# The token sums of the second pair made by VectorE alone, with another table of shifted steps, in a two-layer attention and SwiGLU kernel

## The chip, the core and the metric

The kernel runs on one core of one Trainium2 chip. The metric is the device time of one execution in microseconds (us). Five engines work beside each other on queues of their own: TensorE (PE in the profile; PEld is its weight load), VectorE (DVE), ScalarE (ACT), GpSimd (POOL) and SyncE (SP), which here only issues DMAs.

## What is computed

Two layers, each an attention block with a compressive memory and then a SwiGLU feed-forward block, on 2048 tokens of width 512 in float32. Cut to what matters here:

```python
def _B_ref(x, w_gate, w_up, w_down):      # 512 -> 1792 -> 512
    g = _silu(x @ w_gate)
    u = x @ w_up
    return (g * u) @ w_down
x = x + _A_ref(_layernorm(x), ...)        # attention, four segments of 512 tokens, 32 heads
x = x + _B_ref(_layernorm(x), ...)
x = x + _A_ref(_layernorm(x), ...)
x = x + _B_ref(_layernorm(x), ...)
```

## The kernel before

**Numbers in two parts.** Every operand of a large matmul is held as a rounded part hi and a rest lo; a product is the three matmuls hi·hi, lo·hi and hi·lo, summed in one PSUM bank.

**The feed-forward block** (`ffn`) cuts the 2048 tokens into four blocks of 512 and takes them as two pairs, m = 0 (blocks 0 and 1) and m = 1 (blocks 2 and 3, the "second pair"). The 1792 columns are seven chunks of 256. Chunk 0 is done plainly (`up`, matmuls in line 1039); chunks 1 to 6 are done by a Strassen-Winograd scheme (`strassen`, matmuls in line 1069) that makes seven products in place of eight. Three of its products take the tokens as they are; the other four need sums and differences of token blocks, T0 to T3. These are the **token sums**: `make_t(m)` makes them once for each pair, and all six chunks use them. `down` (matmuls in line 1113, added to the running result in line 1118) multiplies a finished chunk by the down weights.

**The token sums.** `make_t` runs `one(kc)` twice, for the two halves kc of the contraction. Each time it makes T2 (a difference of two parts of block 1 of the pair, three elementwise instructions in `diff`, tiles xn), T0 (three, tiles tt), T1 (two, tile of) and T3 (two, tile tt), all of 128x512 float32 in line 983 for the profile, and then splits each of them in `spl`: ScalarE copies the hi part (line 1004) and VectorE subtracts it to get the lo part (line 1005). `T3E = ("dve", "pool")` says who makes T2: VectorE for the first pair, GpSimd for the second. `strassen` asks for T1 first (`prod(PY, a, 1, tk(1))`, the second product), for T2 two products later. The first matmuls on T1 need its hi part for both kc, the last two its lo part.

**The order of the work.** No engine chooses at run time: each executes its queue in order. The program collects all 13816 operations (`Program.op`) with a price and a due time, `P.prio`; then `issue` runs a list schedule twice (`walk`). In the first walk each engine takes, of its operations whose inputs are ready by the plan, the one with the least due time, the earlier index at a tie. The start that comes out is shifted by `NUDGE[index]` for the operations that the table names, and the second walk takes these as due times and emits the queues. The planner's price of one 512-column VectorE instruction is 512/960 + 0.0687 = 0.602 us; that of a GpSimd token-sum instruction is 1.29 us. It knows no slowdown of one engine by another. All operations of one `make_t(m)` have the same due time, `v + TAT[m]`, so ties go by index: T2, T0, T1, T0's split, T3, then the splits of T1, T3 and T2.

**Around it in the second pair**: block 3 is normed and transposed (line 407; parts hi and lo in lines 411 and 412); its `up` matmuls (line 1039) run while the token sums are made; `down(0, 2)` and `down(0, 3)` (chunk 0 of blocks 2 and 3) have a later due time than the first Strassen chunk; `load_s` prepares the next weights, with sums in line 922 and lo parts in line 936 on GpSimd and hi parts in line 935 on ScalarE. `P.hold` makes the next layer's first norm wait for the VectorE instructions of `make_t(1)`.

Of the kernel before, what the change touches and what calls it, by code (L numbers as in the profile page):

```python
# [24 lines left out]
NB = 3  # L25
CAP = {'pj': 3, 'plt': 3, 'pmx': 3, 'ppv': 3, 'ff': 6, 'st': 6}
LPW = 3
NUDGE = {60: 2.9, 61: -0.9, 124: 0.3, 137: 0.3, 141: -3.3, 171: 4.0, 210: -0.7, 375: 18.2, 377: 15.8, 523: 13.7,
# [7 lines left out]
WOT = ("st", "st", "pj", "pj")  # L36
EARLY_AT = (23, 25, 26)
PAIR, STEP, WAT, TAT = 11.852, 7.441, 15.217, (16.363, 16.627)
T3E = ("dve", "pool")
FIN = 4.95  # L40
WQ1 = -11.849
TA, TF = 15.0, 16.7
# [12 lines left out]
    dve=dict(dve=0.13, act=0.12, pe=0.2, pool=0.17, sp=0.12),  # L55
    pool=dict(pool=0.1, dve=0.14, pe=0.12, act=0.13, sp=0.05),
# [31 lines left out]
class Program:  # L88
# [70 lines left out]
    def issue(self):  # L159
# [11 lines left out]
        for o in self.ops:  # L171
            o.prio = o.start + NUDGE.get(o.index, 0.0)
        self.walk(True)
# [100 lines left out]
def infini_swiglu(ctx: ExitStack, tc: tile.TileContext, x, wq, wk, wv, wo, beta, wg, wu, wd, out,  # L274
# [4 lines left out]
    pool = ctx.enter_context(tc.tile_pool(name="sb", bufs=1))  # L279
# [6 lines left out]
    def sb(tag, shape, dtype=F32, ring=1):  # L286
        return P.buf(pool, tag, shape, dtype, ring)
# [14 lines left out]
    def act(n, fn, reads, writes, sbuf=False, table=None):  # L302
        op("act", n / 1200 + (0.093 if sbuf else 0.05), fn, reads, writes).table = table

    def dve(n, fn, reads, writes, fast=1):
        op("dve", n / 960 / fast + 0.0687, fn, reads, writes)

    def gp(cost, fn, reads, writes):
        op("pool", cost, fn, reads, writes)
# [559 lines left out]
    def ffn(base, x_in, x_out, slots, T):  # L869
# [97 lines left out]
        def make_t(m):  # L967

            (h0, l0), (h1, l1) = XT[2 * m], XT[2 * m + 1]
            R = [sb(slots[f"t{k}"], [128, 2, 4, 2, 128], F32R) for k in range(4)]  # L970
            TT.update(enumerate(R))

            def one(kc):
                half = lambda b, k: (b, lambda: b.ap[:, :, 2 * k + kc].bitcast(F32))
                raws = {}

                def tmp(tag):
                    raw = sb(tag, [128, 4, 128])
                    return raw, lambda: raw.ap

                def ew(eng, f, out, x, y):
                    g = nc.vector if eng == "dve" else nc.gpsimd
                    fn = lambda: getattr(g, f)(out[1](), x[1](), y[1]())  # L983
                    if eng == "dve":
                        dve(512, fn, [x[0], y[0]], [out[0]])
                    else:
                        gp(1.29, fn, [x[0], y[0]], [out[0]])

                def diff(k, eng, tags, ha, la, a, hb, lb, b):
                    d, r = tmp(tags[0]), tmp(tags[1])  # L990
                    ew(eng, "tensor_sub", d, half(ha, a), half(hb, b))
                    ew(eng, "tensor_sub", r, half(la, a), half(lb, b))
                    ew(eng, "tensor_add", r, r, d)
                    raws[k] = r

                def less(k, tag, ha, la, a, j):
                    r = raws[k] = tmp(tag)
                    ew("dve", "tensor_sub", r, half(ha, a), raws[j])
                    ew("dve", "tensor_add", r, r, half(la, a))

                def spl(k):
                    b, r = raws[k]
                    hi, lo = [lambda a=a: R[k].ap[:, a, :, kc] for a in range(2)]
                    act(512, lambda: nc.scalar.copy(hi(), r()), [b], [(R[k], (0, kc))], sbuf=True)  # L1004
                    dve(512, lambda: nc.vector.tensor_sub(lo(), r(), hi().bitcast(F32)),  # L1005
                        [b, (R[k], (0, kc))], [(R[k], (1, kc))])
                diff(2, T3E[m], ("xn_2", "xn_3"), h1, l1, 1, h1, l1, 0)
                diff(0, "dve", ("tt_0", "tt_1"), h1, l1, 0, h0, l0, 0)
                less(1, "of", h1, l1, 1, 0)
                spl(0)  # L1010
                less(3, "tt_0", h0, l0, 1, 1)
                for k in (1, 3, 2):
                    spl(k)
            one(0)
            one(1)

        nup, last = [0], []
# [252 lines left out]
```

## Time and profile before

| | us |
|---|---|
| median of 3 runs | 1867.84 |
| lowest and highest run | 1866.89, 1871.88 |
| the profiled execution | 1871.46 |
| its span, first to last instruction | 1869.7 |
| PE busy | 1822.9 |
| DVE busy | 1407.8 |
| POOL busy | 931.9 |

The profiled execution lies 1.76 us over its own span and 3.62 us over the median of the three runs. Rows of the trace give times from the start of the span. A timeline row gives the start, the time from the start of the first to the end of the last instruction that it merges, the engine, the line and, in brackets, how long the engine sat idle before and whom it waited for.

### The profile page before, as it was taken

To read this page: it belongs to the slowest core of one execution; us is meant where nothing else is said; L and a number is where in the kernel's file an instruction comes from. 1 tells how busy PE (TensorE), PEld (TensorE's weight loads), DVE (VectorE), ACT (ScalarE), POOL (GpSimd) and SP (SyncE) were. 2 spreads that over 40 slices of the span, in tenths; PEclk is the share of its full clock that TensorE was granted. 3 is DMA by queue.
4 is the path that set the end of the run, shared out by engine and by line. 5 is a ranking of instruction groups with operands and counts; after the bars stand their busy time and mean duration, and the time that the engine had idled before them with its cause. 6 is when DMAs were issued, how large, how long until landed. Compare 5 with 4: busy or idle time off the path is not lost.

```text
span 1869.7 us, 33023 instructions
## 1 busy us (share of the span) xinstructions
PE 1822.9 (97%) x11360; PEld 1450.5 (78%) x11360; DVE 1407.8 (75%) x3822; ACT 870.1 (47%) x1629; POOL 931.9 (50%) x1196
## 2 busy tenths in 40 slices
PE   7999999999999999999999999999999999989999
PEld 5787787877778877888877878777777788868887
DVE  6878788788876669766786777887898765786656
ACT  4565564555533343434345655555554433333432
POOL 6344444444655556646533444454345646464551
PEclk9999999999999999999999999999999999999999
DMA  7435444464232122111373354455642312321111
GB/s 240 145 103 148 140 133 141 145 207 128 74 119 63 45 84 92 57 51 52 102 237 103 104 165 117 128 173 146 201 110 76 116 47 58 95 68 51 45 57 46
DMA packets 126967, 206.14 MB, mean 110 GB/s; under 512 B 14160, under 2 KB 52048, under 8 KB 126800
## 3 DMA queue, kind: packets, MB, share of 16 engines
q1 hardware_dynamic: 124752, 203.49, 36.5%
q8 instruction: 91, 1.49, 0.4%
q10 hardware_dynamic: 2048, 0.53, 0.1%
q14 instruction: 76, 0.62, 0.1%
HBM read 136.34 MB, written 67.11 MB: 109 GB/s over the span
## 4 chain that ended last, share of the span: by engine, by line
PE 81%; DVE 9%; DMA 3%; issue 2%; POOL 2%; ACT 2%; SPq 1%; DVEq 0%; POOLq 0%; ACTq 0%
PE ps L1069 24%; PE ps L315 16%; PE ps L1113 15%; PE ps L578 8%; PE ps L629 7%; PE ps L656 7%; PE ps L1039 2%; DVE tt L983 1%; DVE junk L584 1%; PE ps L407 1%; DVE s L1005 1%; PE ps L710 1%; DMA ck<-scrk 1%; DVE s L1118 1%; DMA s<-nm 1%
## 5 line engine op out<-in xcount | busy, mean ns | idle before, releaser
L1069 PE MATMUL ps<-s,s 128*128 128x512 f32 x2016 | 542.5, 396 | 11.9 <-ACT s L1004 6.9
L315 PE MATMUL ps<-s,s 128*128 128x512 f32 x1536 | 523.1, 407 | 3.5 <-ACT s L471 1.8
L584 DVE CUSTOM_DVE_ANT_0 junk<-ps,amask 128x128 bf16<-128x128 f32 (+3 forms) x1024 | 433.9, 484 | 42.2 <-PE ps L578 40.6
L1069 PEld LDWEIGHTS ps<-s,s 128*128 128x128 f32 x2016 | 376.5, 188 | 107.1 <-ACT s L1004 8.7
L1113 PE MATMUL ps<-s,vt 128*128 128x512 f32 x1296 | 376.6, 397 | 1.1 <-ACT vt L1025 1.1
L315 PEld LDWEIGHTS ps<-s,s 128*128 128x128 f32 x1536 | 286.9, 190 | 52.7 <-issue 6.4
L635 ACT ACTIVATE s<-ps 128x512 f32<-128x512 f32 x448 | 254.2, 611 | 107.7 <-PE ps L629 95.8
L1113 PEld LDWEIGHTS ps<-s,vt 128*128 128x128 f32 x1296 | 245.6, 190 | 58.0 <-ACT vt L1025 1.5
L578 PE MATMUL ps<-ck,s 127*128 127x256 f32 (+2 forms) x1024 | 279.3, 334 | 4.4 <-DMA ck<-scrk 1.1
L629 PE MATMUL ps<-s,ck 128*128 128x256 f32 x1280 | 252.1, 288 | 4.1 <-DMA s<-nm 2.5
L629 PEld LDWEIGHTS ps<-s,ck 128*128 128x128 f32 x1280 | 220.7, 189 | 36.8 <-issue 3.9
L1118 DVE TENSOR_TENSOR s<-s,ps 128x512 f32<-128x512 f32 x224 | 149.8, 682 | 95.1 <-PE ps L1113 94.9
L639 POOL TENSOR_SCALAR_AFFINE_SELECT s<-s 128x512 f32<-128x512 f32 x192 | 128.2, 669 | 172.2 <-ACT s L635 169.6
L578 PEld LDWEIGHTS ps<-ck,s 127*128 127x128 f32 x1024 | 178.4, 189 | 28.4 <-issue 4.4
L936 POOL TENSOR_TENSOR s<-mem,s 128x512 fp32r<-128x512 f32 x96 | 130.0, 1354 | 0.2 <-ACT s L935 0.2
L1039 PE MATMUL ps<-s,s 128*128 128x512 f32 x384 | 122.2, 399 | 0.4 <-ACT s L411 0.4
L943 POOL COPY turn<-vt 128x1 f32<-128x1 f32 x20 | 3.7, 184 | 237.1 <-DVE vt L1026 237.1
L512 POOL TENSOR_SCALAR s<-raw 128x512 fp32r<-128x512 f32 x64 | 41.0, 640 | 161.1 <-ACT raw L511 159.6
L656 PE MATMUL ps<-s,vt 128*32 128x384 f32 (+3 forms) x1536 | 115.7, 419 | 0.3 <-DVE mx L584 0.2
L656 PEld LDWEIGHTS ps<-s,vt 128*32 128x32 f32 x1536 | 43.4, 109 | 64.7 <-issue 48.0
L635 ACT ACTIVATE pc<-ps 128x512 f32<-128x512 f32 x128 | 79.1, 619 | 20.5 <-PE ps L629 18.8
L514 POOL TENSOR_TENSOR s<-raw,s 128x512 fp32r<-128x512 f32 x64 | 84.0, 1312 | 4.4
(173 smaller groups left out, 2599.2 us busy)
## 6 DMA issues: line engine op xcount, KB each, us to landing
s<-scrq SPq DMA_DIRECT2D x128, 192.0 KB, 3.6
ck<-scrk SPq DMA_DIRECT2D x128, 192.0 KB, 4.5
scrq<-s SPq DMA_DIRECT2D x32, 512.0 KB, 3.9
scrk<-s SPq DMA_DIRECT2D x32, 512.0 KB, 3.4
scrq<-s SPq DMA_DIRECT2D x32, 256.0 KB, 3.3
scrk<-s SPq DMA_DIRECT2D x32, 256.0 KB, 2.4
s<-xmid SPq DMA_DIRECT2D x32, 256.0 KB, 4.7
xin<-xmid SPq DMA_DIRECT2D x32, 256.0 KB, 2.6
```

Source lines behind the costliest of these rows:

```text
L315: pe(n, passes, lambda: nc.tensor.matmul(view(ps.ap), lhsT=av(a.ap), rhs=bv(b.ap), start=start, stop=stop), [(a, rk[0]), (b, rk[1])], [ps])
L578: nc.tensor.matmul(ps.ap[:, a * 256:a * 256 + nk], lhsT=cq.ap[0:127, 2 * j + p, qt * 128:(qt + 1) * 128], rhs=ck.ap[0:127, p, 0:nk], start ...
L584: dve(w, lambda a=a, qt=qt, w=w, ps=ps, junk=junks[qt % 2]: nc.vector.tensor_tensor_reduce(out=junk.ap[:, :w], in0=ps.ap[:, a * 256:a * 25 ...
L629: nc.tensor.matmul(ps.ap[:, 256 * p:256 * p + 256], lhsT=ck.ap[:, p, kt * 128:kt * 128 + 128], rhs=cq.ap.rearrange("r (j p) c -> r p j c", ...
L635: act(512, lambda: nc.scalar.activation(view().rearrange("p x i c -> p (x i c)"), ps.ap, AF.Exp, scale=SCALE), [ps], [(Pb, key)], table="exp")
L639: gp(0.593, lambda: nc.gpsimd.affine_select(out=view()[:, 0], in_=view()[:, 0], pattern=[[0, 4], [1, 128]], compare_op=OP.is_ge, fill=0.0, ...
L656: nc.tensor.matmul(ps.ap[32 * i:32 * i + 32, qt * 128:(qt + k) * 128], lhsT=vt.ap[:, kt, VW * hd:VW * hd + 32], rhs=view(k=k)[:, :, idx], ...
L936: gp(n / 400, lambda hi=hi, lo=lo, src=src: nc.gpsimd.tensor_sub(lo(), src(), hi().bitcast(F32)), [read, (wt, (o0, 0))], [(wt, (o0, 1))])
L1039: pe(512, 1, lambda i=i, j=j, kc=kc, x=x, ps=ps, wt=wt: nc.tensor.matmul(ps.ap, lhsT=wt.ap[:, i, kc, cs], rhs=XT[b][j].ap[:, :, kc], start ...
L1069: pe(512, 1, lambda i=i, kc=kc, x=x, buf=buf, view=view: nc.tensor.matmul(ps.ap, lhsT=w.ap[:, o, i, kc], rhs=view(buf.ap, kc), start=(x == 0),
L1113: pe(512, 1, lambda i=i, j=j, fi=fi, x=x, ps=ps, wt=wt, cs=cs: nc.tensor.matmul(ps.ap, lhsT=ht.ap[:, 0:2048].rearrange("p (f a c) -> p f a ...
L1118: dve(512, lambda ps=ps, t=t: nc.vector.tensor_add(xb.ap[:, t, :], xb.ap[:, t, :], ps.ap), [ps, (xb, t)], [(xb, t)])
```

## The change

All four token sums of the second pair are made by VectorE, as those of the first pair are: the six GpSimd instructions of each `make_t(1)` (three for each kc, twelve in the two layers) become VectorE instructions in the planner's and the engine's queue. The operations and their indices stay the same. The table of shifts is another one: 70 entries in place of 69, with three indices in common (2909, 6986 and 13792). Neither table names an operation of `make_t(1)`. Since a shift changes what the planner puts next, the queues of all engines can differ from the first shifted operation on.

```diff
-NUDGE = {60: 2.9, 61: -0.9, 124: 0.3, 137: 0.3, 141: -3.3, 171: 4.0, 210: -0.7, 375: 18.2, 377: 15.8, 523: 13.7,
...
-         11949: -3.0, 12102: 7.2, 13281: -4.5, 13432: 7.2, 13635: -0.5, 13792: 12.4}
+NUDGE = {74: 4.6, 103: 0.2, 106: -2.3, 127: -8.8, 159: 2.0, 161: 2.9, 194: -0.8, 269: 5.1, 313: 23.9, 370: 1.3,
...
+         11776: -0.5, 11827: 3.5, 12216: 0.7, 12218: 10.1, 12451: 5.3, 13590: 10.5, 13792: 10.4}
-T3E = ("dve", "pool")
+T3E = "dve"
...
-                diff(2, T3E[m], ("xn_2", "xn_3"), h1, l1, 1, h1, l1, 0)
+                diff(2, T3E, ("xn_2", "xn_3"), h1, l1, 1, h1, l1, 0)
```

## Rows read from the trace of the kernel before

**Rows 1.** The page, part 1: busy time and share of each engine.

```profile
PE 1822.9 (97%) x11360; PEld 1450.5 (78%) x11360; DVE 1407.8 (75%) x3822; ACT 870.1 (47%) x1629; POOL 931.9 (50%) x1196
```

**Rows 2.** Busy time by stretch: length, engines, granted clock (PEclk), DMA share, GB/s.

```profile
0.00:60.00 60.00, 45.36 (x197) 35.99 (x198) 39.65 (x135) 28.15 (x51) 32.43 (x56) 0.97 0.71 220
...
715.00:755.00 40.00, 35.93 (x149) 27.87 (x148) 35.86 (x46) 13.25 (x25) 26.61 (x21) 0.91 0.25 86
755.00:925.00 170.00, 170.00 (x743) 137.61 (x742) 117.42 (x189) 68.01 (x120) 95.50 (x114) 1.00 0.21 63
...
1640.00:1680.00 40.00, 34.55 (x149) 27.17 (x148) 35.39 (x46) 13.03 (x24) 26.32 (x21) 0.96 0.22 74
```

**Rows 3.** Timeline of PE around the second pair's first Strassen products, first layer.

```profile
729.35 8.92 PE L1039 MATMUL ps<-s,s 128*128 128x512 f32 x38
...
740.43 0.86 PE L1069 MATMUL ps<-s,s 128*128 128x512 f32 x3
744.22 2.57 PE L1069 MATMUL ps<-s,s 128*128 128x512 f32 x8 [2.93 <-ACT s L1004]
747.55 1.22 PE L1069 MATMUL ps<-s,s 128*128 128x512 f32 x2 [0.76 <-DVE s L1005]
748.57 4.96 PE L1113 MATMUL ps<-s,vt 128*128 128x512 f32 x13
753.37 0.40 PE L1069 MATMUL ps<-s,s 128*128 128x512 f32 x1
```

**Rows 4.** Timeline of PE at the same place of the second layer.

```profile
1665.17 0.85 PE L1069 MATMUL ps<-s,s 128*128 128x512 f32 x3
1668.71 2.13 PE L1069 MATMUL ps<-s,s 128*128 128x512 f32 x8 [2.69 <-ACT s L1004]
1673.17 0.73 PE L1069 MATMUL ps<-s,s 128*128 128x512 f32 x2 [2.32 <-DVE s L1005]
1673.73 4.74 PE L1113 MATMUL ps<-s,vt 128*128 128x512 f32 x13
1678.31 0.40 PE L1069 MATMUL ps<-s,s 128*128 128x512 f32 x1
```

**Rows 5.** Busy time of 2 us behind the waits of the first layer (columns of Rows 2).

```profile
748.00:750.00 2.00, 2.00 (x6) 1.52 (x6) 1.32 (x3) 0.74 (x2) 0.08 (x1) 0.50 0.00 0
```

**Rows 6.** Timeline of DVE around the token sums, first layer, then second layer.

```profile
721.98 0.68 DVE L1026 TENSOR_TENSOR vt<-raw,vt 128x512 fp32r<-128x512 f32 x1
...
725.57 2.61 DVE L983 TENSOR_TENSOR tt<-s,s 128x512 f32<-128x512 f32 x2
728.22 1.67 DVE L983 TENSOR_TENSOR tt<-tt,tt 128x512 f32<-128x512 f32 x1
729.81 1.27 DVE L1118 TENSOR_TENSOR s<-s,ps 128x512 f32<-128x512 f32 x2
...
742.84 0.68 DVE L983 TENSOR_TENSOR of<-of,s 128x512 f32<-128x512 f32 x1
...
744.57 1.78 DVE L983 TENSOR_TENSOR tt<-s,of 128x512 f32<-128x512 f32 x1
746.28 1.22 DVE L1005 TENSOR_TENSOR s<-of,s 128x512 fp32r<-128x512 f32 x1
...
1650.31 2.38 DVE L983 TENSOR_TENSOR tt<-s,s 128x512 f32<-128x512 f32 x2
...
1667.33 0.68 DVE L983 TENSOR_TENSOR of<-of,s 128x512 f32<-128x512 f32 x1
```

**Rows 7.** Timeline of POOL in the same stretch.

```profile
727.71 1.63 POOL L983 TENSOR_TENSOR xn<-xn,xn 128x512 f32<-128x512 f32 x1
...
743.15 0.95 POOL L936 TENSOR_TENSOR s<-phik,s 128x256 fp32r<-128x256 f32 x1 [3.19 <-ACT s L935]
```

**Rows 8.** Group by line, POOL's subtractions of the token sums: busy, mean ns, idle before.

```profile
L983 POOL TENSOR_TENSOR xn<-s 128x512 f32<-128x512 f32 x8 | 13.7, 1713 | 13.3 <-ACT s L1004 10.0 <-ACT s L411 2.8 <-DVE s L412 0.3
```

**Rows 9.** Timeline of PE in the first pair, first layer: the wait for a token sum.

```profile
539.63 1.66 PE L1069 MATMUL ps<-s,s 128*128 128x512 f32 x6 [0.65 <-ACT s L1004]
```

12 rows, old and new, of the table NUDGE are left out of this document.

## The prediction

> **What bounds the kernel now.** I read the page's busy shares first: TensorE is busy 97% of the span, the next engine 75% [rows 1]. So the end is set by TensorE's work and by what little it idles, 1869.7 - 1822.9 = 46.8 us. The busy time by stretch then says where that idle time lies: 14.6 us at the start (60.00 - 45.36), 4.1 us in the 40 us around the second pair's token sums of the first layer, 5.5 us in the same stretch of the second layer, and nothing in the 170 us that follow [rows 2]. Because TensorE is full behind it, a microsecond won in one of these stretches is a microsecond off the end. The same rows show a second thing: the granted clock is 1.00 in the full stretch, but 0.91 and 0.96 in the two with the token sums. So those stretches cost more than their idle time.
>
> **What the two stretches cost.** I take the timeline of TensorE there. With full queues a matmul of 512 columns, 0.40 us long, starts every (8.92 - 0.40)/37 = 0.230 us, from the 38 at 729.35 [rows 3]. In the first layer three matmuls from 740.43 are through their issue at 741.12; TensorE then waits for ScalarE's hi part of T1, later for VectorE's lo part of it, and reaches the matmul at 753.37. In those 12.25 us it issued 8 + 2 + 13 = 23 matmuls, worth 5.29 us: 7.0 us are lost [rows 3]. In the second layer the same count from 1665.86 to 1678.31 gives 12.45 - 5.29 = 7.2 us [rows 4]. Part of it is not waiting: behind the waits of the first layer the granted clock is 0.50, the lower of the two levels, 1.2 in place of 2.4 GHz, and the matmuls of the down product run at half pace until it rises [rows 5]; in the second layer the stretch has 0.96 [rows 2]. Together the two places hold 14.1 us (6.96 + 7.16), 0.75% of the span.
>
> **Why T1 is late.** Next the timeline of VectorE. It is busy for 35.9 of the 40 us [rows 2]. T1's last sum for kc = 1 begins at 742.84 as the 22nd instruction of the row, 17.27 us after the first [rows 6]. Two undisturbed instructions of 0.68 us, the pair at 729.81, take 1.27 us together [rows 6], so one starts some 0.60 us after the other, and 21 starts need 12.6 us. The other 4.7 us are in instructions that ran while GpSimd made T2: 2.61 us for two and 1.67 us for one that takes 0.68 us alone [rows 6], beside GpSimd's 1.63 us from 727.71 on [rows 7]. In the second layer the 22nd instruction begins at 1667.33, 17.02 us after the first, an excess of 4.4 us [rows 6]. After that, T3's sum and T1's lo part take 1.78 and 1.22 us [rows 6] beside GpSimd's weight work, which starts at 743.15 [rows 7] and stays.
>
> **The change part by part.**
> *Removed:* twelve GpSimd instructions, of which the eight subtractions alone are 13.7 us, of an engine half idle [rows 1, 8]. By themselves they are worth nothing; what goes with them is VectorE's excess of 4.7 and 4.4 us.
> *Added:* six VectorE instructions in each layer ahead of T1, because T2 has the lower index: 6 x 0.60 = 3.6 us. They stand before the two additions of line 1118 and before the split of block 3's activations; those come at most 3.6 us later by count and about 1 us earlier in time. Net on VectorE's chain: T1's hi part comes 4.7 - 3.6 = 1.1 us earlier in the first layer and 0.8 us in the second. ScalarE's copies and the next layer's first norm wait for the same last instruction as now, so `P.hold` costs nothing.
> *The plan:* this is the larger part. By its own prices the planner had T1's hi part ready for TensorE at 725.57 + 12.6 + (744.22 - 742.84) = 739.6 [rows 3, 6], before TensorE was done with its other work at 741.1, so it saw no gap and put nothing into it; on the chip it came at 744.2. After the change the planner expects 739.6 + 3.6 = 743.2, and its 0.602 us is the chip's 0.60 us with GpSimd out of the way. It sees 2.1 us missing and fills them, nine matmuls, with what is ready. There is plenty: the down product of chunk 0 for block 2 is 48 matmuls, 11 us, and its last input is written at 721.98 + 0.68 us [rows 6]. Then T1's hi part no longer stalls TensorE. If that cover were absent, 2.1 us of waiting would stay, plus the clock.
> *What is late next:* T1's lo part, behind T3's sum and GpSimd's weight work. Its bounds are 0 (the fill also moves the lo part's matmuls back) and the 2.32 us that TensorE waited for it in the second layer [rows 4]. The nearest row is the first pair, where VectorE makes all four sums already and TensorE waits 0.65 us [rows 9]; I take 1.0 us in each layer, and no fall of the clock.
> Sum of this part: 7.0 + 7.2 - 2 x 1.0 = 12.1 us off (from 14.1).
>
> What the trace shows of the two engines together is that VectorE's sums of two SBUF tiles take 1.67 to 1.78 us beside GpSimd and 0.68 us alone [rows 6, 7]. The Trainium skill has a rule for it in "SBUF — State Buffer", section "Who interferes with whom": a VectorE instruction with two SBUF inputs contends with a GpSimd instruction that reads SBUF, and one with a single SBUF input does not. That speaks against the change too, since all instructions that it gives to VectorE are of the contending kind and GpSimd's weight work remains; the second rival below is priced for that.
>
> *The table.* No shift, old or new, is on an operation of `make_t(1)`, but the queues are drawn anew from the first one. The trace of before shows no row for the new order. The bounds come from what there is to win or lose: in the first 60 us TensorE idles 14.6 us [rows 2], of which no order removes the wait for the first rows; I allow 5 us of gain there and in the small waits of the rest. A loss has a price in [rows 3, 4]: a wait of some 3 us that pulls the clock down costs 7 us. I take 0, as nothing in the rows tells one table from the other.
>
> **From span to time.** The sum is against the profiled 1871.46 us, which lies 3.62 us over the median of the three runs; the runs spread by 5 us. Against its own time the change gives 1871.5 - 12.1 = 1859.4; against the median 1867.84 - 12.1 = 1855.7. Since a profiled execution that is slower than the median may have lost more to the clock than the others did, I take 1 us less of gain: 1857.
>
> **The rivals.**
> *1. The forecast:* both stalls go but for about 1 us, the table is neutral: 1857, own range 1853 to 1862. Chance 0.45.
> *2. The contention moves on.* GpSimd's weight work meets the longer row of VectorE sums, T1's lo part stays 2.3 us late in each layer and the clock still falls, which costs the 7.2 - 2.69 - 2.32 = 2.2 us of the second layer [rows 4]: 14.1 - 2 x 4.5 = 5.1 us won, 1863. For it: the 1.78 and 1.22 us beside the weight work [rows 6]. Against it: the planner's fill moves the matmuls on T1 back by 2.1 us. Chance 0.2. The skill's rule named above would give this case if all the remaining GpSimd instructions met a VectorE sum.
> *3. The table also mends the start and the rest:* 12 + 5 us, 1851. Against it: the rows give no reason. Chance 0.15.
> *4. Slower: the new order opens stalls elsewhere.* Outside the first 60 us and the two stretches TensorE idles only 46.8 - 14.6 - 4.1 - 5.5 = 22.6 us in 1730 us now, in many small pieces [rows 1, 2]; an order that lets it wait some 3 us at a place would drop the clock and cost 7 us there, as in [rows 3, 4]. Two such places eat the 12 us; with the third the kernel is slower than before, 1867.8 - 12 + 21 = 1877. Chance 0.13.
> *5. Nothing comes of it:* the stall hangs on something else (ScalarE's copies or the transposes of block 3) and the times stay near 1867. Against it: T1's last sum ends at 743.52, 0.70 us ahead of the matmul that waits for its copy [rows 3, 6]. Chance 0.07.
>
> **How the numbers follow.** The measurement can tell about 0.3%, 5.6 us, from no change, so faster means under 1862.2 and slower over 1873.4. Cases 1 and 3 are faster almost wholly (0.43 and 0.15), case 2 in a few of its outcomes (0.05): 0.63. Case 4 is slower in nearly all, 0.12. The rest, 0.25, is within. The range is from 1848 (case 3 with its bound) to 1869 (cases 2 and 5): it leaves out case 4 and a little of case 3.
>
> **What would show it.** In the profile after: no GpSimd instruction in line 983; VectorE's sums of the second pair at 0.60 us from start to start, the 22 instructions up to T1 plus six in about 16.3 us; matmuls of line 1113 between the `up` matmuls and the first ones on T1; TensorE waits of line 1069 for lines 1004 and 1005 under 1 us there; and a clock of 1.00 in both stretches. I am wrong if TensorE still waits more than 2 us there, if the clock still falls, or if idle time elsewhere grows by more than 5 us.

## The result, and the profile after

The changed kernel takes 1871.87 us (median of 12 runs, 1869.66 to 1878.13) beside 1867.64 us for the kernel before on the same chip (12 runs, 1865.81 to 1871.88). The ratio is 1.0023, interval 1.0012 to 1.0034: 4.2 us slower, inside the 0.3% that the prediction called the same. I had forecast 1857, with a range up to 1869: wrong.

The profiled execution of after took 1870.86 us, 1.0 us under its median; that of before lay 3.8 us over its own. So the two traces show spans that are nearly equal (1869.1 and 1869.7) where the medians differ by 4.2, and a stretch may look a few us better here than it is.

The line of the page of after with the busy time by engine, beside [rows 1]:

```profile
PE 1821.3 (97%) x11360; PEld 1448.1 (77%) x11360; DVE 1402.0 (75%) x3834; ACT 872.0 (47%) x1629; POOL 918.3 (49%) x1184
```

TensorE still bounds the kernel and idles 1869.1 - 1821.3 = 47.8 us, where it idled 46.8 before. Busy time by stretch of after, the first, second, third and last as in [rows 2] (length, then busy time and instructions of PE, PEld, DVE, ACT and POOL, the granted clock, DMA share and GB/s):

```profile
0.00:60.00 60.00, 44.47 (x205) 35.66 (x206) 40.97 (x141) 28.48 (x52) 34.12 (x56) 0.97 0.72 220
715.00:755.00 40.00, 37.30 (x164) 28.94 (x163) 38.39 (x60) 15.49 (x28) 19.48 (x21) 1.00 0.30 99
755.00:925.00 170.00, 170.00 (x742) 137.26 (x741) 115.16 (x188) 66.44 (x116) 96.25 (x114) 1.00 0.23 67
925.00:985.00 60.00, 51.77 (x248) 41.86 (x247) 45.11 (x147) 23.85 (x42) 22.38 (x24) 0.97 0.61 185
1120.00:1240.00 120.00, 116.94 (x966) 93.37 (x968) 93.52 (x353) 65.87 (x130) 51.47 (x80) 1.00 0.45 126
1640.00:1680.00 40.00, 38.06 (x170) 29.98 (x169) 38.34 (x58) 16.22 (x29) 18.63 (x19) 1.00 0.21 73
```

Two of these stretches stand in no row ahead of the prediction. In before they are:

```profile
925.00:985.00 60.00, 55.35 (x268) 44.65 (x267) 48.26 (x151) 22.82 (x42) 24.40 (x29) 1.00 0.66 207
1120.00:1240.00 120.00, 118.94 (x993) 94.76 (x993) 94.79 (x358) 65.40 (x130) 51.97 (x80) 1.00 0.46 133
```

The two stretches with the token sums are better. TensorE issues 164 and 170 matmuls in 40 us where it issued 149 in each, at a clock of 1.00 instead of 0.91 and 0.96. At 0.230 us each the 15 and 21 more are 3.5 and 4.8 us. The loss is elsewhere: 20 matmuls fewer and 3.6 us more idle time in the 60 us where the first layer passes into the second (925 to 985), with the clock at 0.97, and 27 fewer (they are of several sizes) and 2.0 us more idle time in the second layer's attention from 1120 to 1240.

The timeline of PE in after at the place of [rows 3], and its one longest wait at the place of [rows 4] (start, length, count; in brackets the idle time before and its releaser):

```profile
740.71 3.14 PE L1113 MATMUL ps<-s,vt 128*128 128x512 f32 x13
...
747.53 0.51 PE L1069 MATMUL ps<-s,s 128*128 128x512 f32 x1 [1.11 <-DVE s L1005]
747.87 1.92 PE L1113 MATMUL ps<-s,vt 128*128 128x512 f32 x7
750.60 0.50 PE L1069 MATMUL ps<-s,s 128*128 128x512 f32 x1 [0.81 <-ACT tt L1084]
...
1679.12 0.50 PE L1069 MATMUL ps<-s,s 128*128 128x512 f32 x1 [1.24 <-DVE s L1005]
```

The down product (L1113) now stands ahead of the products of T1; the wait for ScalarE's hi part (2.93 and 2.69 us) is gone and the one for VectorE's lo part is 1.11 and 1.24. The timeline of DVE there, beside [rows 6]:

```profile
722.43 1.27 DVE L983 TENSOR_TENSOR xn<-s 128x512 f32<-128x512 f32 x2
...
739.38 0.69 DVE L983 TENSOR_TENSOR of<-of,s 128x512 f32<-128x512 f32 x1
740.10 1.67 DVE L983 TENSOR_TENSOR tt<-s,of 128x512 f32<-128x512 f32 x1
741.69 1.79 DVE L1026 TENSOR_TENSOR vt<-raw,vt 128x512 fp32r<-128x512 f32 x1
```

```profile
739.43 1.78 POOL L936 TENSOR_TENSOR s<-mem,s 128x512 fp32r<-128x512 f32 x1
```

T1's last sum, at 739.38, is the 29th instruction from the first row on and begins 16.95 us after it: 28 steps of 0.605 us, the undisturbed pace. The slow instructions begin at 740.10, behind the first long instruction of GpSimd's weight work (739.43, in the second block). POOL has twelve instructions fewer, and none in line 983.

Now the place where TensorE waits longest behind the start in after, the passage to the second layer. The timeline of POOL first (L512 is the rounding of a tile that is then stored to `scrk`, a scratch tensor in DRAM, and read back as `ck`), then of DVE at that time, then the wait on PE, and busy time by stretch behind it:

```profile
932.74 4.07 POOL L512 TENSOR_SCALAR s<-raw 128x512 fp32r<-128x512 f32 x1 [2.02 <-ACT raw L511]
```

```profile
932.64 0.68 DVE L1026 TENSOR_TENSOR vt<-of,vt 128x512 fp32r<-128x512 f32 x1
...
935.65 0.68 DVE L1026 TENSOR_TENSOR vt<-tt,vt 128x512 fp32r<-128x512 f32 x1
936.25 1.27 DVE L1118 TENSOR_TENSOR s<-s,ps 128x512 f32<-128x512 f32 x2
```

```profile
948.35 1.24 PE L578 MATMUL ps<-ck,s 127*128 127x256 f32 x4 [4.55 <-DMA ck<-scrk]
```

```profile
946.00:950.00 4.00, 1.65 (x6) 1.49 (x7) 0.96 (x5) 0.00 (x0) 0.06 (x1) 0.83 1.01 318
950.00:955.00 5.00, 5.00 (x25) 4.27 (x24) 4.05 (x19) 1.22 (x3) 0.00 (x0) 0.79 0.63 219
```

From 932.64 on VectorE runs six instructions with two SBUF inputs back to back, at its full pace, and GpSimd's one instruction lasts as long as they do: it ends at 936.81, 0.5 us after the last of them (936.33), when VectorE has turned to sums with a PSUM input (L1118). The store to `scrk` and the load of `ck` wait for it, TensorE waits 4.55 us for `ck` (0.8 us in before), and the granted clock is 0.83 and 0.79 behind the wait. With the old shifts the same instruction takes 1.07 us (e8, below). The Trainium skill, "SBUF — State Buffer", section "Who interferes with whom", says that these two kinds contend and that the order of issue decides which of them blocks; the trace agrees in that GpSimd, which began 0.10 us after a VectorE sum, is the one that stands still, with 4.07 us here. That it stands still for six instructions is what the trace adds. The prediction had weighed the rule only for VectorE as the one that is slowed.

### The profile page after: what moved, and what is told of

Read it like the earlier page. It is cut to its first block, busy times and chain, and to the rows that moved or that the text cites. A ratio compares the mean times of both kernels' runs of the same rounds, so it can differ in the third digit from the quotient of the medians.

```text
span 1869.1 us, 33022 instructions
## 1 busy us (share of the span) xinstructions
PE 1821.3 (97%) x11360; PEld 1448.1 (77%) x11360; DVE 1402.0 (75%) x3834; ACT 872.0 (47%) x1629; POOL 918.3 (49%) x1184
## 5 line engine op out<-in xcount | busy, mean ns | idle before, releaser
L1069 PEld LDWEIGHTS ps<-s,s 128*128 128x128 f32 x2016 | 375.6, 188 | 102.8 <-DVE tt L1082 3.5
L1113 PE MATMUL ps<-s,vt 128*128 128x512 f32 x1296 | 377.6, 396 | 0.2 <-DVE s L1118 0.2
L315 PEld LDWEIGHTS ps<-s,s 128*128 128x128 f32 x1536 | 285.9, 189 | 53.5 <-issue 5.3
L1113 PEld LDWEIGHTS ps<-s,vt 128*128 128x128 f32 x1296 | 243.6, 188 | 57.3 <-DVE s L1118 1.2
L1118 DVE TENSOR_TENSOR s<-s,ps 128x512 f32<-128x512 f32 x224 | 150.1, 683 | 94.9 <-PE ps L1113 94.7
L512 POOL TENSOR_SCALAR s<-raw 128x512 fp32r<-128x512 f32 x64 | 44.7, 699 | 163.4 <-ACT raw L511 155.0
L1039 PEld LDWEIGHTS ps<-s,s 128*128 128x128 f32 x384 | 71.6, 188 | 19.5 <-ACT s L411 2.0
```

The lines of the kernel that those rows point to most:

```text
L315: pe(n, passes, lambda: nc.tensor.matmul(view(ps.ap), lhsT=av(a.ap), rhs=bv(b.ap), start=start, stop=stop), [(a, rk[0]), (b, rk[1])], [ps])
L1039: pe(512, 1, lambda i=i, j=j, kc=kc, x=x, ps=ps, wt=wt: nc.tensor.matmul(ps.ap, lhsT=wt.ap[:, i, kc, cs], rhs=XT[b][j].ap[:, :, kc], start ...
L1069: pe(512, 1, lambda i=i, kc=kc, x=x, buf=buf, view=view: nc.tensor.matmul(ps.ap, lhsT=w.ap[:, o, i, kc], rhs=view(buf.ap, kc), start=(x == 0),
L1113: pe(512, 1, lambda i=i, j=j, fi=fi, x=x, ps=ps, wt=wt, cs=cs: nc.tensor.matmul(ps.ap, lhsT=ht.ap[:, 0:2048].rearrange("p (f a c) -> p f a ...
L1118: dve(512, lambda ps=ps, t=t: nc.vector.tensor_add(xb.ap[:, t, :], xb.ap[:, t, :], ps.ap), [ps, (xb, t)], [(xb, t)])
```

## The experiments

**The two halves of the change, each alone, and the empty table.** e1_vector_old_table is the move alone:

```diff
-T3E = ("dve", "pool")
+T3E = "dve"
...
-                diff(2, T3E[m], ("xn_2", "xn_3"), h1, l1, 1, h1, l1, 0)
+                diff(2, T3E, ("xn_2", "xn_3"), h1, l1, 1, h1, l1, 0)
```

> The changed kernel with the table of shifts of before: only the engine of T2 is changed. If the engine move is worth what the prediction says and the new table took it back, this is 10 to 12 us faster than before (ratio about 0.994) and 14 us faster than the changed kernel. If the move is worth only what its own two stretches show in the two traces and the rest is run-to-run, 3 to 7 us faster (0.997). If the old table suits the old order alone, no faster than before (1.000 to 1.002).

Measured: 1864.73 us (11 runs), ratio to before 0.9983, interval 0.9974 to 0.9991.

e2_pool_new_table is the table alone:

```diff
-NUDGE = {60: 2.9, 61: -0.9, 124: 0.3, 137: 0.3, 141: -3.3, 171: 4.0, 210: -0.7, 375: 18.2, 377: 15.8, 523: 13.7,
...
+NUDGE = {74: 4.6, 103: 0.2, 106: -2.3, 127: -8.8, 159: 2.0, 161: 2.9, 194: -0.8, 269: 5.1, 313: 23.9, 370: 1.3,
...
```

> The kernel of before with the new table: only the table is changed. If the table is what took the gain back, this is slower than before by the sum of the gain and the 4 us that were measured: 10 to 16 us (ratio 1.006 to 1.009). If the table is neutral and the move itself brings nothing, 0 to 4 us slower. The stalls of the second pair should stand in its trace as in before, with the clock at half speed behind them.

Measured: 1872.71 us, ratio 1.0021, interval 1.0010 to 1.0031. Its two stretches of the token sums:

```profile
715.00:755.00 40.00, 37.20 (x162) 29.50 (x161) 38.75 (x57) 15.70 (x29) 26.32 (x23) 0.96 0.25 86
1640.00:1680.00 40.00, 36.88 (x159) 29.18 (x159) 36.66 (x53) 15.76 (x29) 24.16 (x20) 0.96 0.20 73
```

e3_vector_no_table and e4_pool_no_table have no shifts, and T2 on VectorE and on GpSimd:

```diff
-NUDGE = {60: 2.9, 61: -0.9, 124: 0.3, 137: 0.3, 141: -3.3, 171: 4.0, 210: -0.7, 375: 18.2, 377: 15.8, 523: 13.7,
...
+NUDGE = {}
```

> VectorE makes T2 and the table is empty. It prices both tables against none on this side: if the new table is as good as the old one was for the old order, this is 4 to 15 us slower than the changed kernel; if the new table does nothing, it equals the changed kernel within 3 us.

> GpSimd makes T2 and the table is empty: the difference to the empty table with VectorE is the worth of the move with no table in play. The prediction's mechanism gives 12 us; if the move is worth 3 to 7 us, that is what stands between the two.

Measured: e3 1874.46 us, ratio 1.0037 (1.0025 to 1.0049); e4 1879.76 us, ratio 1.0066 (1.0054 to 1.0078). The medians together (those of the kernel before, in the sets of runs that are used here, lie between 1867.56 and 1868.12, so a difference of under 1 us tells nothing):

| T2 made by | no table | old table | new table |
|---|---|---|---|
| GpSimd | 1879.76 | 1867.64 | 1872.71 |
| VectorE | 1874.46 | 1864.73 | 1871.87 |
| the move | -5.3 | -2.9 | -0.8 |

The move gains with the old table and with none; with the new one the runs can't tell a gain (ratios to before 1.0021 and 1.0023). The new table costs 5.1 us more than the old on GpSimd's kernel and 7.1 us on VectorE's (3.9 and 7.5 us by the ratios), and outweighs the move. With the new table there is also less for the move to win: GpSimd's kernel then issues 162 and 159 matmuls in the two stretches (e2), where [rows 2] have 149 and 149. Of the cases named ahead of the runs, e1 lies at the lower edge of its second (3 to 7 us), e2 between its two, and e3 in its second: 2.6 us over the changed kernel, so there the new table does little more than none, while the old one is worth 9.7 us.

**e5_before_again**, the kernel before once more, for a second trace of it:

> The kernel of before, unchanged, profiled once more, to see how much one place of it varies from execution to execution. If the waits for T1 cost the same every time, its two stretches lose 7.0 and 7.2 us again. If the fall of the clock behind them varies, they lose anything from 3.5 (the waits alone) to 7 us each, and the profile the prediction was made from was a dear one.

Measured: 1869.03 us (one run). Busy time at the start and in the second layer's token sums, and TensorE's waits there:

```profile
0.00:60.00 60.00, 45.86 (x217) 36.63 (x221) 42.31 (x147) 30.04 (x55) 33.64 (x58) 0.97 0.71 221
...
1640.00:1680.00 40.00, 35.96 (x155) 28.37 (x154) 36.55 (x47) 13.54 (x26) 26.33 (x22) 0.96 0.22 78
```

```profile
1667.93 3.55 PE L1069 MATMUL ps<-s,s 128*128 128x512 f32 x8 [2.69 <-ACT s L1004]
1672.39 0.73 PE L1069 MATMUL ps<-s,s 128*128 128x512 f32 x2 [0.91 <-DVE s L1005]
```

The hi wait is 2.69 us again, but the lo wait is 0.91 where [rows 4] have 2.32, and the stretch holds 155 matmuls, six more than in [rows 2], 1.4 us. The first layer's has 149 in both traces, with waits of 2.91 and 0.65 us. The execution on which I built was a dear one, and not only here: in its first 60 us TensorE issued 197 matmuls [rows 2], where it issued 217 this time.

**The new table, cut by the index of the operation** (VectorE makes T2 in all). e6_vector_new_then_old has the new shifts below 6700 and the old ones from there:

```diff
-         6720: 4.3, 6816: 30.3, 6860: 1.9, 6986: 2.5, 7002: -0.7, 7168: 2.6, 7344: -4.4, 7842: 0.6, 7933: 2.9,
...
+         6749: 4.7, 6760: -9.2, 6790: 3.2, 6851: -26.0, 6886: 2.7, 6953: -4.1, 6986: 2.9, 7003: 9.0, 7054: -0.0,
...
```

> VectorE makes T2; the new table's entries for operations under 6700 (the first layer up to its last feed-forward chunk) and the old table's from there on. By equal progress of TensorE in the profiles, the changed kernel was 6.8 us ahead of before shortly ahead of the seam between the layers, and the old table gives another 5 us from there. If the loss is in the new table's shifts from the seam on, this is 1861 to 1863 us. If the seam eats whatever lead TensorE brings, it loses that lead at 925 to 970 us and ends at 1865 to 1868 us.

e7_vector_old_then_new is the reverse, the old shifts below 6700:

```diff
-NUDGE = {74: 4.6, 103: 0.2, 106: -2.3, 127: -8.8, 159: 2.0, 161: 2.9, 194: -0.8, 269: 5.1, 313: 23.9, 370: 1.3,
...
+NUDGE = {60: 2.9, 61: -0.9, 124: 0.3, 137: 0.3, 141: -3.3, 171: 4.0, 210: -0.7, 375: 18.2, 377: 15.8, 523: 13.7,
...
```

> The other half: the old table's entries under 6700 and the new table's from there on. If the new shifts from the seam on cost the gain, this is as slow as the changed kernel or slower, 1871 to 1875 us. If the first half decides, it is near the old table's 1865 us.

Measured: e6 1863.78 us (1861.23 to 1864.97), ratio 0.9974 (0.9964 to 0.9984), the lowest median of all (its interval overlaps those of e1 and of e10, below) and faster than both kernels; e7 1872.07 us, ratio 1.0026 (1.0016 to 1.0035). The loss is in the new shifts from 6700 on.

e8_vector_new_old_seam is the changed kernel with the old shifts for 6700 to 7100, the passage to the second layer:

```diff
-         6720: 4.3, 6816: 30.3, 6860: 1.9, 6986: 2.5, 7002: -0.7,
+         6749: 4.7, 6760: -9.2, 6790: 3.2, 6851: -26.0, 6886: 2.7, 6953: -4.1, 6986: 2.9, 7003: 9.0, 7054: -0.0,
```

> The changed kernel with the shifts on operations 6700 to 7100 alone (the last chunk of the first layer and the first projections of the second) taken from the old table. If those five new entries make the wait for the keys at 944 to 948 us, this is 5 to 6 us faster than the changed kernel, 1866 us, and equal to the new-then-old table up to the second layer's attention. If they don't, it stays at 1871 to 1872 us.

Measured: 1868.63 us, ratio 1.0002 (0.9993 to 1.0011), 3.2 us under the changed kernel. Its profiled execution is the shortest of its runs, 3.8 us under the median. The timeline of POOL, of DVE and of PE at the passage, and busy time by stretch:

```profile
934.10 1.07 POOL L512 TENSOR_SCALAR s<-raw 128x512 fp32r<-128x512 f32 x1 [2.52 <-ACT raw L511]
935.25 1.62 POOL L514 TENSOR_TENSOR s<-raw,s 128x512 fp32r<-128x512 f32 x1
```

```profile
933.99 0.68 DVE L1026 TENSOR_TENSOR vt<-of,vt 128x512 fp32r<-128x512 f32 x1
...
935.62 1.80 DVE L459 TENSOR_TENSOR s<-phik,s 128x512 fp32r<-128x512 f32 x1
```

```profile
946.24 0.48 PE L578 MATMUL ps<-ck,s 127*128 127x256 f32 x2 [1.10 <-DMA ck<-scrk]
```

```profile
925.00:985.00 60.00, 55.73 (x274) 45.05 (x273) 51.10 (x169) 24.63 (x44) 21.98 (x25) 1.00 0.61 199
```

Here GpSimd gets in: L512 takes 1.07 us, VectorE is the one that is slowed (1.80 us beside L514), and TensorE waits 1.10 us for `ck` in place of 4.55. The stretch holds 274 matmuls, where before has 268 and after 248. Why GpSimd gets in behind one VectorE sum here and only behind six in after, though it begins 0.1 us after the start of a sum in both, no run shows.

It is not the accident of one execution, and it does not hang on the move. The two other kernels with the new shifts of the passage have the held instruction too, e2 (where GpSimd makes T2) and e7:

```profile
938.08 4.07 POOL L512 TENSOR_SCALAR s<-raw 128x512 fp32r<-128x512 f32 x1 [2.04 <-ACT raw L511]
```

```profile
936.18 4.07 POOL L512 TENSOR_SCALAR s<-raw 128x512 fp32r<-128x512 f32 x1 [2.03 <-ACT raw L511]
```

There TensorE waits 2.7 and 2.8 us for `ck`. In the eight traces with the old shifts of the passage the instruction takes 1.06 or 1.07 us and the wait is 0.8 to 1.6 us. Without any shifts it is held as well, 5.24 us in e3 and 4.04 us in e4 (line 505 in these two), with waits of 2.5 and 2.2 us.

e11_vector_new_attention is e6 with the new shifts from 7100 to 10000:

```diff
-         7490: -5.3, 7735: 7.4, 7940: 0.9, 8469: 3.3, 8608: 2.5, 8763: -1.3, 8986: 10.2, 9088: -17.5, 9335: 16.8, 9759: 1.3,
+         7168: 2.6, 7344: -4.4, 7842: 0.6, 7933: 2.9, 8249: 6.3, 8359: 2.2, 8974: -1.0, 9211: 2.3, 9246: 3.5, 9710: 1.0,
```

> VectorE makes T2; the table is that of e6_vector_new_then_old (new shifts below operation 6700, old ones from there) except for the shifts from 7100 to 10000, which are the new table's: the first half of the second layer's attention alone. Theory (the new shifts cost some 3 to 4 us within the attention of the second layer): at equal TensorE progress the run loses 2 to 4 us against e6 between 1000 and 1400 us and keeps it, and the median comes out near 1867 against 1863.8. Rival (the loss of e8 against e6, 4.9 us in the median, comes from the shifts above 10000, of the attention's second half and the second MLP): no loss there, the median stays within 1 us of e6.

Measured: 1868.59 us, ratio 1.0001 (0.9993 to 1.0010), 4.8 us over e6: as much as e8 loses against e6 (4.9 us). Busy time from 1120 to 1240 in e6, then in e11, and three of the waits on PE in e11:

```profile
1120.00:1240.00 120.00, 118.83 (x994) 94.89 (x993) 93.89 (x354) 65.82 (x130) 51.80 (x81) 1.00 0.47 133
```

```profile
1120.00:1240.00 120.00, 117.20 (x982) 93.26 (x981) 92.68 (x347) 65.82 (x130) 50.28 (x78) 1.00 0.44 126
```

```profile
1065.41 0.65 PE L578 MATMUL ps<-ck,s 127*128 127x256 f32 x3 [1.62 <-DMA ck<-scrk]
...
1128.63 0.50 PE L315 MATMUL ps<-s,s 128*128 128x512 f32 x1 [0.47 <-DVE s L412]
...
1197.16 0.50 PE L315 MATMUL ps<-s,s 128*128 128x512 f32 x1 [0.92 <-DVE mem L718]
```

From 1120 to 1240 TensorE idles 2.8 us with the new shifts (e11) and 3.1 us in after, 1.2 us with the old ones (e6) and 1.1 us in before. No wait there is long and the clock stays at 1.00: it is a handful of waits under 1 us, most of them for VectorE. The same handful (0.9 us for line 718, 0.8 to 1.0 us for line 584, 0.5 to 0.7 us for line 412, and 0.5 to 0.6 us for ScalarE's line 635) stands in the traces of all five kernels with these new shifts (after, e2, e7, e8, e11); the waits for lines 718 and 412 stand in none of the six traces with the old ones. With it TensorE idles 1.6 us (e11 beside e6) or 2.0 us (after beside before) longer there, less than half of the 4.8 us. The 1.62 us for `ck` at 1065 add to it in e11 alone.

**Refill or contention.** The prediction took the planner's refill of TensorE's queue for the larger part of the move. A price in the plan changes the order and not who computes, so each part can be had alone. In e9_pool_priced_later GpSimd keeps T2, and the first VectorE sum of each half (the first one of T0, from which T1 is made) is priced 1.8 us dearer; TensorE's order is then that of e1, in the traces for all 11360 matmuls by line, tiles and shape:

```diff
-                        dve(512, fn, [x[0], y[0]], [out[0]])
+                        dve(ew.n, fn, [x[0], y[0]], [out[0]])
...
-                    d, r = tmp(tags[0]), tmp(tags[1])
+                    ew.n, d, r = 512 + 1730 * (m == 1 and k == 0), tmp(tags[0]), tmp(tags[1])
...
+                    ew.n = 512; ew(eng, "tensor_sub", r, half(la, a), half(lb, b))
```

> The kernel before with its own table and with GpSimd making T2, but the planner charges 1.8 us more for the first VectorE sum of T1 in each half (one price in the plan, 2.40 in place of 0.60 us; no instruction is added, left out or given to another engine). TensorE's order comes out the same as in e1_vector_old_table, so this is the refill of TensorE's queue alone, with the contention of VectorE and GpSimd left in. Theory, as predicted (the refill is the larger part): T1's hi part still comes late on the chip, but the matmuls ahead of it cover most of it; TensorE's wait for ScalarE's hi part falls from 2.93 and 2.69 us to under 1.2 us in both layers, the clock falls less, and the median lies 1.5 to 2.5 us under the kernel before (the whole move is worth 2.9 with this table), some 1865.7. Rival (taking the contention away is the larger part): the late VectorE still holds TensorE up by 2 us or more at the hi or the lo part, and the median is within 1 us of the kernel before, some 1867.

Measured: 1868.54 us beside 1868.12 us for before, ratio 1.0006 (0.9997 to 1.0015). Busy time by stretch, and the waits on PE:

```profile
715.00:755.00 40.00, 35.41 (x153) 28.10 (x152) 37.40 (x48) 13.65 (x25) 27.09 (x21) 0.96 0.28 92
...
1640.00:1680.00 40.00, 35.49 (x151) 28.26 (x150) 36.27 (x46) 14.22 (x26) 25.52 (x20) 0.91 0.23 80
```

```profile
751.11 0.79 PE L1069 MATMUL ps<-s,s 128*128 128x512 f32 x1 [4.22 <-DVE s L1005]
...
1674.78 0.79 PE L1069 MATMUL ps<-s,s 128*128 128x512 f32 x1 [4.07 <-DVE s L1005]
```

e10_vector_priced_zero is the mirror: VectorE makes T2 as in e1, but these sums are priced at nothing, and TensorE's order is that of before, again for all 11360 matmuls:

```diff
-                        dve(512, fn, [x[0], y[0]], [out[0]])
+                        dve(ew.n, fn, [x[0], y[0]], [out[0]])
...
-                    d, r = tmp(tags[0]), tmp(tags[1])
+                    ew.n, d, r = -60 if m == 1 and k == 2 else 512, tmp(tags[0]), tmp(tags[1])
...
-                    raws[k] = r
+                    ew.n, raws[k] = 512, r
```

> The mirror of the last one: VectorE makes T2 with the old table (e1_vector_old_table), but the planner charges nothing for these twelve sums. TensorE's order comes out the same as in the kernel before, so this is the contention taken away alone, without the refill. Theory, as predicted: T1's hi part comes some 1 us earlier than in the kernel before (4.7 - 3.6 and 4.4 - 3.6 us), and TensorE waits for it 1.5 to 2.2 us in both layers in place of 2.93 and 2.69, with some fall of the clock behind it; the median is within 1.5 us of the kernel before, some 1866.6. Rival (the contention is the larger part): the waits are under 1 us each and the median lies 2 to 3 us under the kernel before, as in e1, some 1865.

Measured: 1864.47 us beside 1868.12 us, ratio 0.9982 (0.9973 to 0.9991). The same two views:

```profile
715.00:755.00 40.00, 37.07 (x166) 29.15 (x165) 37.48 (x60) 13.92 (x25) 19.21 (x20) 1.00 0.27 92
...
1640.00:1680.00 40.00, 37.52 (x161) 29.53 (x160) 34.70 (x53) 15.48 (x29) 16.87 (x14) 0.96 0.20 67
```

```profile
742.74 2.91 PE L1069 MATMUL ps<-s,s 128*128 128x512 f32 x10 [2.50 <-ACT s L1004]
...
1662.86 4.41 PE L1069 MATMUL ps<-s,s 128*128 128x512 f32 x10 [1.90 <-ACT s L1004]
```

And e1, for the corner of the square that is left: the two stretches, its waits for T1, and T1's last sum of the first layer beside GpSimd's weight work:

```profile
715.00:755.00 40.00, 37.06 (x166) 29.15 (x165) 39.07 (x57) 14.39 (x26) 21.99 (x16) 1.00 0.27 92
1640.00:1680.00 40.00, 37.19 (x168) 29.70 (x168) 37.41 (x55) 15.94 (x29) 19.89 (x15) 1.00 0.22 76
```

```profile
751.13 0.50 PE L1069 MATMUL ps<-s,s 128*128 128x512 f32 x1 [2.31 <-DVE s L1005]
...
1672.46 0.50 PE L1069 MATMUL ps<-s,s 128*128 128x512 f32 x1 [2.36 <-DVE s L1005]
```

```profile
741.94 1.67 DVE L983 TENSOR_TENSOR of<-of,s 128x512 f32<-128x512 f32 x1
```

```profile
741.27 1.79 POOL L936 TENSOR_TENSOR s<-mem,s 128x512 fp32r<-128x512 f32 x1
```

| | TensorE's order | T2 made by | matmuls in the two stretches | waits for T1, hi and lo, in each layer (us) | ratio to before |
|---|---|---|---|---|---|
| before | its own | GpSimd | 149, 149 | 3.69, 5.01 | 1 |
| before again (e5) | its own | GpSimd | 149, 155 | 3.56, 3.60 | 1 |
| e9 | refilled | GpSimd | 153, 151 | 4.22, 4.07 | 1.0006 |
| e10 | that of before | VectorE | 166, 161 | 2.50, 1.90 | 0.9982 |
| e1 | refilled | VectorE | 166, 168 | 2.31, 2.36 | 0.9983 |

The refill alone brings nothing: the hi wait goes, and TensorE stops a few matmuls later for the lo part, 4.22 and 4.07 us. Taking GpSimd out of VectorE's way alone brings as much as the whole move. The waits for T1 say the same: 7.2 to 8.7 us in the two layers together while GpSimd makes T2, 4.4 and 4.7 us when VectorE does, in either order. The theory of the prediction fell here; its rival is the nearer one on the time (3.7 us under before, where it had 2 to 3), but not on e10's waits, which it had put under 1 us each: hi waits of 2.50 and 1.90 us stay, and what goes is the lo wait.

## Why the prediction was wrong, step by step

*What bounds the kernel, and what the change does in its place:* right. TensorE is busy 97% as before; VectorE makes 0.605 us a step and has T1's last sum begun after 16.95 us (28 steps; some 16.3 us for 27 expected); the down product stands ahead of T1's products; both stretches have a clock of 1.00.

*"What the two stretches cost", 7.0 + 7.2 us:* too much, being read from one execution. The second look at before loses 1.4 us less in the second layer. In the step *from span to time* I took off 1 us for this and put it down to the clock; a part of the excess is at the start, far from the change, where e5 issues 20 matmuls more in 60 us. The profiled times of before and e1 differ by 1871.46 - 1862.71 = 8.8 us where the medians differ by 2.9: the one lies 3.8 us over its median, the other 2.0 under. The matmul counts follow the profiled times (17 + 19 more in e1, 8.3 us), so the traces show more than a usual run gains.

*"The plan: this is the larger part":* failed. Alone it is worth 4 and 2 matmuls, 0.9 and 0.5 us, against the trace of [rows 2] (4 and -4 against e5), and nothing in the median. The contention alone is worth 17 and 12 matmuls, 3.9 and 2.8 us (17 and 6 against e5), and 3.7 us in the median. I had given it only the 1.1 and 0.8 us by which the hi part comes earlier, and had not seen that the lo part's wait (0.76 and 2.32 us in [rows 3, 4]) hangs on it too: e10 has none.

*What is late next, 1.0 us a layer:* the right wait, undersized. The move alone leaves 2.31 and 2.36 us (e1), all of the 2.32 that was the upper bound. After waits 1.11 and 1.24 us for the lo part, and 0.81 us more in the first layer for line 1084. The second rival, contention that moves on to the weight work, came true in its wait, T1's lo part 2.3 us late in each layer: in e1 T1's last sum takes 1.67 us beside the weight work, in after T3's sum takes 1.67 us. It had a fall of the clock with it, which did not come, in e1 or in after.

*The sum, 12.1 us:* 15 + 21 = 36 matmuls, 8.3 us, against the first trace of before. In medians, 2.9 us with the old table, and with the new one nothing that the runs can tell (0.8 us).

*The table, taken as 0:* the step that decided. It costs 5.1 to 7.1 us; I had the price of one bad wait (7 us) and gave it no weight in the forecast. In medians, each against the kernel named before it: the move 1867.64 to 1864.73 (-2.9), the new early shifts to 1863.78 (-1.0, less than the runs can tell), the new shifts from 7100 on to 1868.63 (+4.9, which e11 puts between 7100 and 10000), those of the passage to 1871.87 (+3.2).

*The rivals:* beside the second, the fourth, an order that opens stalls elsewhere, is what happened in kind, with 0.13. It had counted three waits of 3 us with a fall of the clock; there is one, of 4.55 us, and the rest that the traces show are small ones. The sign that I had named was there: idle time outside the start and the two stretches went from 46.8 - 14.6 - 4.1 - 5.5 = 22.6 us to 47.8 - 15.5 - 2.7 - 1.9 = 27.7 us, 5.1 more.

*What stays open:* which shift between 7100 and 10000 makes TensorE wait in the attention, and where the larger part of the 4.8 us goes; the runs only place the loss. The 3.2 us of the passage rest on shifts that were changed together. The held GpSimd instruction and the long wait for `ck` go together in all thirteen traces, and no run held the one without the other: that the one makes the other is argued from this and from the sizes (3.0 us longer than in e8 the one, 3.45 us the other). Where the usual run of e1 spends the 2.0 us that its profiled run saved, no trace shows. The granted clock is a hint: over its eleven runs the mean is 0.9979, in the profiled one 0.999, and 0.0011 of 1861 us is 2.0 us (an estimate).

## What to carry to other kernels

Where VectorE and GpSimd both sum from SBUF, look at each meeting of a long row of the one with a short instruction of the other: either can be the one that stands still, and it matters who waits for it. A new order of a full schedule is a change of its own; price it from the places that have a store and a load behind them, and not at nothing. To learn whether an engine's speed or the plan's order makes a gain, change a price in the plan alone: it gives the order of the one kernel on the engines of the other.

## What the runs showed of the hardware

A row of VectorE sums at full pace can hold a GpSimd instruction for the length of the row: L512 takes 4.07 us in after, e2 and e7, and 1.07 us in e8. It need not: in e8 it got in behind one sum of such a row.

Behind waits of like length the clock does not always fall. In the first layer of e10, TensorE waits 2.50 us and the stretch has a clock of 1.00; in the second it waits 1.90 us and the stretch has 0.96. In the first layer of before it waits 2.93 and 0.76 us, and the stretch has 0.91 [rows 2, 3]. In e1 it waits 2.31 and 2.36 us, and both stretches have 1.00.
